# Attention and feed-forward on one core: block order, reciprocals in the products' bank, and a new order table

## The chip, the core and the metric

The kernel runs on one core of one Trainium2 chip. The metric is the device time of one execution in microseconds (us), lower is better. The core has a matrix engine (TensorE, PE in the profile, with its weight loads as PEld), a vector engine (VectorE, DVE), a scalar engine (ScalarE, ACT), a general engine (GpSimd, POOL) and a queue engine that issues the transfers (SyncE, SP). Each engine runs its own instructions in the order in which the program wrote them, and waits on semaphores for the others. Matrix products land in PSUM banks of 128 x 512 floats.

## What is computed

Causal attention in blocks of 64 positions over 8 batches, 8 heads, 576 positions and 64 dimensions, then a feed-forward layer with a SiLU over 4608 tokens (512 -> 2048 -> 512):

```python
scores = scale * np.matmul(q, k.transpose(0, 1, 3, 2))
mask = block_i >= block_j                     # blocks of 64 positions
scores = np.where(mask, scores, -1000000000.0)
attn = np.exp(scores - np.max(scores, axis=-1, keepdims=True))
attn = attn / (np.sum(attn, axis=-1, keepdims=True) + 1e-09)
attn_out = np.matmul(attn, v)
...
h = x @ w_in                                  # x: (4608, 512)
g = h * (1.0 / (1.0 + np.exp(-h)))
return (g @ w_out).astype(np.float32)
```

The feed-forward weights arrive as 64-bit words, which the kernel turns into 32-bit floats itself.

## The kernel before

**Precision.** Every operand of a large product is held as an upper part and a remainder (names ending in `hi` and `lo`); a product is three matmuls, or two where one side is left whole. ACT makes the upper parts, POOL mostly the remainders.

**Work items.** The feed-forward layer is cut into 18 blocks of 256 tokens. A step (block, d) has two items of 12 matmuls for the first layer (`ffn1`, line 599) and, two steps later, two items of 6 matmuls for the second (`ffn2`, line 629); between them ACT takes `silu` and `g_hi`, and POOL `g_lo`. The table's word `ffn` stands for one item. Blocks 0 and 1 hold the first 128 positions, which `First` (a, b) and `Second` (c0 to c3) attend to with small matmuls; while weights still come in, the two blocks alternate, `EVEN` times a step of each (`steps`, lines 657 to 659). Block 0 collects its output in PSUM bank S2 and in the bank U (line 622); both are needed by the units below.

**Weights.** 32 tiles w0 to w31: a transfer, `rebias` on ACT, three `bits` on DVE (lines 208, 212, 216), `hi` on ACT, `lo` on POOL.

**Units.** 64 units, one for a batch and head. `scores` fills the banks S0 to S2 (line 289); `max`, `max2` (DVE) find the row maxima; `sub` (DVE) subtracts them and so frees S0 to S2 for the next unit; `exp` and `p_hi` (ACT), `p_lo` (POOL); `sums` (DVE); `pv` multiplies by the values into the one bank U (line 370); `lower` (ACT) and `fold` (DVE, line 381) add its halves into `xu`. For a pair of units, at the odd one, `sums2` (DVE) makes the reciprocals `rr` and spreads them over 448 columns with a 32 x 32 transpose into `u.rb`, the upper half of the SBUF tile MR (lines 355 to 363); `mult` (line 384) multiplies `xu` by them, and `x_hi` (ACT, line 401) and `x_lo` (POOL, line 405) cut the result into the feed-forward tiles `x`. Block k from 4 on is ready once the last pair of the batches that it spans is.

**Order.** All of this is written into the engines' queues in one order. Up to unit 16 it is the table `ORDER`, one word for a method; 60 words `ffn` stand ahead of `u0.scores`, 152 in all. From unit 17 on the loop at line 722 takes over: in step i it writes `scores` and `max` of unit i, `fold` of unit i-2, `max2`, the splits of unit i+1, then for a pair `mult`, `x_hi`, `x_lo` of unit i-2, then `ffn(pace - 3)` (four items as a rule), `sums` and `pv` of unit i-1, the rest of unit i, and `ffn(3)`. After unit 63 nothing but feed-forward items is left.

Of the kernel before, what the change touches and what calls it, by code (L numbers as in the profile page):

```python
# [55 lines left out]
w2.hi w3.bits:2 w2.lo ffn w4.bits:0 w3.hi c0.load w4.bits:1 b.hi:0 w3.lo w5.rebias w7.load w4.bits:2 ffn b.hi:1 b.lo:0 w6.rebias
w8.load w5.bits:0 w4.hi ffn w5.bits:1 w4.lo b.lo:1 w5.bits:2 ffn silu w6.bits:0 g_hi w9.load w5.hi w6.bits:1 c0.scores:0 g_lo
w7.rebias w6.bits:2 ffn w7.bits:0 w5.lo w10.load silu w7.bits:1 w6.hi ffn w7.bits:2 w8.rebias w6.lo c0.max:0 w7.hi w11.load
w8.bits:0 ffn w9.rebias w8.bits:1 w7.lo g_hi w8.bits:2 ffn w10.rebias g_lo w9.bits:0 w8.hi w12.load w9.bits:1 ffn w8.lo w9.bits:2
c0.sub:0 w9.hi w13.load w10.bits:0 ffn silu w10.bits:1 w9.lo w11.rebias w10.bits:2 c0.scores:1 w12.rebias w11.bits:0 g_hi w14.load  # L60
ffn w10.hi w11.bits:1 w11.bits:2 w10.lo ffn w12.bits:0 w11.hi w15.load w12.bits:1 g_lo w13.rebias c0.max:1 ffn w12.bits:2 w11.lo
w14.rebias w13.bits:0 w12.hi w16.load ffn c0.sub:1 silu w13.bits:1 w12.lo w15.rebias ffn w13.bits:2 g_hi w14.bits:0 w13.hi
w17.load w14.bits:1 ffn w13.lo w14.bits:2 c0.exp w15.bits:0 ffn w18.load g_lo w15.bits:1 c0.sum ffn w15.bits:2 silu c0.norm ffn
w16.rebias w19.load w17.rebias w16.bits:0 w14.hi ffn g_hi w16.bits:1 w14.lo w16.bits:2 c0.turn:0 ffn w17.bits:0 g_lo w20.load
c0.back:0 w17.bits:1 w15.hi c1.load c0.turn:1 w18.rebias w17.bits:2 w15.lo ffn c0.back:1 w18.bits:0 w21.load w16.hi w18.bits:1
c0.pv silu w16.lo w18.bits:2 w19.rebias ffn g_hi w22.load w19.bits:0 w18.hi w17.hi w19.bits:1 ffn w20.rebias w19.bits:2 w17.lo
c0.hi w20.bits:0 w23.load ffn c0.lo g_lo w21.rebias w20.bits:1 w20.bits:2 c1.scores:0 w18.lo silu w21.bits:0 w19.hi w24.load ffn
w21.bits:1 w22.rebias w19.lo w21.bits:2 g_hi ffn w22.bits:0 w25.load g_lo w23.rebias w22.bits:1 w20.hi ffn w22.bits:2 w21.hi
w20.lo w23.bits:0 w22.hi w26.load w23.bits:1 ffn w21.lo w23.bits:2 w24.rebias silu ffn w24.bits:0 w22.lo w25.rebias w24.bits:1
g_hi ffn w24.bits:2 w26.rebias c1.max:0 w23.hi w28.load w25.bits:0 ffn w27.load w25.bits:1 w23.lo c1.sub:0 ffn w25.bits:2 g_lo  # L70
w26.bits:0 w29.load c1.scores:1 w26.bits:1 silu ffn g_hi c1.max:1 w24.hi g_lo w26.bits:2 w27.rebias ffn w27.bits:0 w30.load w24.lo
c1.sub:1 silu c1.load_v ffn w27.bits:1 w25.hi w26.hi w27.bits:2 w25.lo w28.rebias ffn w27.hi w31.load w28.bits:0 w26.lo w28.bits:1
ffn c1.exp w30.rebias ffn c1.sum g_hi w29.rebias g_lo ffn w28.bits:2 w29.bits:0 c1.norm ffn w29.bits:1 w29.bits:2 silu ffn
w30.bits:0 w29.hi w27.lo w30.bits:1 c1.turn:0 w30.bits:2 ffn c1.back:0 c3.load w30.hi c1.turn:1 c2.load ffn c1.back:1 w31.rebias
c1.pv w28.hi w31.bits:0 g_hi w28.lo ffn w31.bits:1 c1.hi c2.load_v w31.bits:2 g_lo c1.lo ffn silu c3.scores:0 w31.hi g_hi ffn
c3.max:0 g_lo c3.sub:0 c2.scores:0 w29.lo silu ffn c2.max:0 w30.lo c2.sub:0 c3.scores:1 ffn c3.max:1 c3.sub:1 c2.scores:1 ffn
c2.max:1 u0.load c3.exp c2.sub:1 ffn c3.load_v g_hi c3.sum c2.exp g_lo ffn c2.sum c3.norm ffn silu ffn g_hi c2.norm c3.turn:0 ffn
c3.back:0 u0.split_hi g_lo c3.turn:1 c2.turn:0 ffn w31.lo c2.back:0 c2.turn:1 ffn c2.back:1 c3.back:1 c2.pv ffn c2.hi u0.split_lo
c3.pv ffn c3.hi silu u1.load c3.lo ffn output c2.lo u0.load_v g_hi u0.scores g_lo output ffn mask u0.max silu u1.split_hi ffn g_hi
u0.max2 u0.v_hi g_lo ffn u1.split_lo silu ffn u0.sub ffn g_hi u2.load g_lo u1.scores store u0.exp:0 u0.v_lo u0.exp:1 ffn u1.max  # L80
u0.p_hi:0 store u0.exp:2 u0.p_lo:0 ffn u1.load_v u2.split_hi u1.max2 ffn u0.p_hi:1 u2.split_lo output ffn u1.sub silu ffn
u0.p_hi:2 u0.p_lo:1 output u0.sums u3.load g_hi u2.scores u0.p_lo:2 ffn g_lo u2.max u1.exp:0 u0.pv u1.exp:1 u3.split_hi u2.max2
ffn u1.exp:2 u3.split_lo u0.lower ffn u1.p_hi:0 u1.p_hi:1 u2.sub u1.v_hi ffn u1.v_lo u0.fold silu u3.scores u1.p_lo:0 u1.sums
u2.load_v g_hi u4.load u1.p_hi:2 u1.p_lo:1 ffn u3.max u1.p_lo:2 ffn u2.exp:0 g_lo u3.max2 u2.exp:1 u1.pv u2.exp:2 u4.split_hi ffn
u2.p_hi:0 u3.sub u4.split_lo u1.lower ffn u1.fold silu ffn u1.sums2 g_hi u2.p_lo:0 u5.load u2.p_hi:1 u4.scores u2.v_hi g_lo
u2.p_hi:2 ffn u2.p_lo:1 u1.mult silu u2.sums u1.x_hi u2.v_lo ffn u5.split_hi u2.p_lo:2 u3.load_v u4.max store ffn g_hi g_lo u2.pv
u4.max2 u3.exp:0 u1.x_lo u3.exp:1 ffn u3.exp:2 u3.p_hi:0 u5.split_lo u2.lower u3.sums ffn silu ffn u2.fold u3.p_hi:1 u3.p_lo:0
u4.sub u6.load g_hi u3.p_hi:2 ffn g_lo u3.v_hi u3.sums2 u5.scores u3.v_lo silu u3.p_lo:1 u4.load_v ffn u3.p_lo:2 u4.exp:0 u5.max
u6.split_hi ffn u4.exp:1 u6.split_lo u3.pv u4.exp:2 u5.max2 ffn u3.lower u4.p_hi:0 u3.fold u4.p_hi:1 ffn u7.load u4.p_lo:0 u5.sub
u4.v_hi u4.p_hi:2 store u4.v_lo ffn u3.mult u4.p_lo:1 u5.load_v u4.sums u6.scores u3.x_hi u4.p_lo:2 g_hi ffn u6.max u7.split_hi  # L90
g_lo u5.exp:0 ffn u5.exp:1 u3.x_lo u5.exp:2 u6.max2 u4.pv u7.split_lo ffn u5.p_hi:0 u6.sub u4.lower u5.p_hi:1 ffn u5.p_lo:0
# [713 lines left out]
```

## Time and profile before

| | |
|---|---|
| median of 3 runs | 1060.84 us (1060.02 to 1061.04) |
| profiled execution | 1061.71 us, of which the span from first to last instruction is 1060.0 us |
| PE busy | 1033.0 us (97%) |
| DVE, POOL, ACT busy | 792.0 us (75%), 750.6 us (71%), 746.3 us (70%) |
| granted TensorE clock | 0.992 of full speed over the span |

The program has four stretches. Until 26.8 us the first weights and a and b are made, and no feed-forward item has begun. From there to 133.5 us weights are turned and blocks 0 and 1 run. From 133.5 us to 319.75 us the table interleaves units 0 to 16 with items; after it comes the loop, and from 930 us on items alone. In the profile a busy PE need not be PE at its best: a matmul that waits for its operands while the one before it is still in flight is shown as a longer one. What PE lost is therefore read as the length of a stretch less the matmuls in it at their pace in an undisturbed stretch.

### The profile page before, as it was taken

Reading aid. Unit: us, or ns where it says so; the run is one execution under the profiler, and the core shown is the slowest. Engines: PE = TensorE matmul, PEld = TensorE weight load, DVE = VectorE, ACT = ScalarE, POOL = GpSimd, SP = SyncE. Lnnn points to the kernel's source line nnn. Section 1 sums busy time; section 2 is a strip of 40 time slices with the busy share of each in tenths; the row PEclk is TensorE's granted clock in tenths of the full one; section 3 lists DMA queues with packets and bytes.
Section 4 is the critical chain, followed back from the end, with each engine's and each line's share of the span. In section 5 each row is a group of like instructions: output and inputs, shape, how many; then the busy total and the mean of one; then the engine's idle time right before and its main releaser. Section 6 shows DMA issues by size and latency. Waiting matters only on the chain.

```text
span 1060.0 us, 19884 instructions
## 1 busy us (share of the span) xinstructions
PE 1033.0 (97%) x6996; PEld 930.3 (88%) x6996; DVE 792.0 (75%) x2238; ACT 746.3 (70%) x1193; POOL 750.6 (71%) x721
## 2 busy tenths in 40 slices
...
DMA packets 35043, 79.93 MB, mean 75 GB/s; under 512 B 4736, under 2 KB 12928, under 8 KB 34944
## 3 DMA queue, kind: packets, MB, share of 16 engines
...
## 4 chain that ended last, share of the span: by engine, by line
PE 77%; DVE 11%; POOL 4%; ACT 3%; DMA 3%; issue 2%; SPq 0%; DVEq 0%; POOLq 0%; ACTq 0%
PE h L599 31%; PE o L629 30%; PE S L289 7%; PE U L370 7%; DVE Mx L233 1%; DMA qkraw<-in_qk_dram 1%; DVE wm L216 1%; DVE S L212 1%; POOL pl L344 1%; DVE S L208 1%; DVE Dx L233 1%; DVE xu L384 1%; DMA wst<-in_moe_w_in_dram 1%; POOL ql L267 1%; POOL qh L265 1%
## 5 line engine op out<-in xcount | busy, mean ns | idle before, releaser
L599 PE MATMUL h<-x,wi 128*128 128x256 f32 x3456 | 440.5, 282 | 0.9 <-ACT g L606 0.9
L599 PEld LDWEIGHTS h<-x,wi 128*128 128x128 f32 x3456 | 429.0, 189 | 13.4 <-ACT g L606 2.7
L629 PE MATMUL o<-wo,g 128*128 128x512 f32 x1680 | 425.0, 398 | 2.7 <-ACT ot L637 2.7
L629 PEld LDWEIGHTS o<-wo,g 128*128 128x128 f32 x1680 | 305.9, 188 | 66.7 <-ACT ot L637 4.3
L344 POOL TENSOR_TENSOR pl<-p,ph 128x448 fp32r<-128x448 f32 (+1 forms) x192 | 227.2, 1209 | 85.5 <-ACT ph L336 85.5
L617 POOL TENSOR_TENSOR g<-g,g 128x512 fp32r<-128x512 f32 x144 | 186.2, 1293 | 127.9 <-ACT g L612 121.2
L233 DVE TRANSPOSE_TENSOR_REDUCE Mx<-S 64x4 f32<-64x128 f32 (+4 forms) x384 | 135.5, 404 | 76.6 <-PE S L289 76.1
L606 ACT ACTIVATE g<-h 128x512 f32<-128x512 f32 x144 | 86.0, 598 | 98.2 <-POOL g L617 56.8
L233 DVE TRANSPOSE_TENSOR_REDUCE Dx<-p 128x14 f32<-128x448 f32 (+3 forms) x320 | 123.3, 445 | 1.3 <-ACT p L330 1.2
L612 ACT CAST g<-g 128x512 fp32r<-128x512 f32 x144 | 89.3, 620 | 47.4 <-PE o L629 45.2
L330 ACT ACTIVATE p<-T 128x512 f32<-128x512 f32 (+1 forms) x192 | 105.0, 604 | 9.3 <-POOL ph L346 8.7
L265 POOL TENSOR_TENSOR qh<-qkraw,qh 64x576 fp32r<-64x576 f32 x64 | 95.2, 1488 | 17.9 <-ACT qh L261 10.9
L336 ACT CAST ph<-p 128x512 fp32r<-128x512 f32 (+1 forms) x192 | 104.2, 595 | 0.4 <-PE U L370 0.3
L289 PE MATMUL S<-qh 128*128 128x448 f32 (+3 forms) x320 | 92.6, 302 | 2.2 <-DVE T L319 1.0
L606 ACT ACT_TABLE_LOAD x66 | 84.7, 1283 | 1.2
L289 PE MATMUL S<-ql,qh 128*128 128x448 f32 (+3 forms) x320 | 84.1, 307 | 0.5 <-POOL ql L267 0.5
L330 ACT ACT_TABLE_LOAD x62 | 79.5, 1283 | 6.5 <-DVE Dx L233 5.3
L267 POOL TENSOR_TENSOR ql<-qkraw,qh 128x448 fp32r<-128x448 f32 x64 | 76.9, 1202 | 8.5 <-PE S L575 3.5
L401 ACT CAST x<-xu 128x256 fp32r<-128x256 f32 (+3 forms) x80 | 22.6, 339 | 81.7 <-DVE xu L384 81.7
L370 PE MATMUL U<-ph,vc 128*128 128x448 f32 (+3 forms) x320 | 74.6, 298 | 2.2 <-POOL vc L276 2.2
L321 DVE TENSOR_TENSOR T<-S,MR 128x256 f32<-128x256 f32 (+2 forms) x192 | 73.2, 408 | 0.0
L261 ACT CAST qh<-qkraw 128x1024 fp32r<-128x1024 f32 x64 | 66.8, 1044 | 2.8 <-DMA qkraw<-in_qk_dram 2.6
...
## 6 DMA issues: line engine op xcount, KB each, us to landing
qkraw<-in_qk_dram SPq DMA_DIRECT2D x128, 256.0 KB, 3.9
...
```

What stands on the lines that cost most here:

```text
L233: nc.vector.tensor_reduce(out=out, in_=in_, axis=AX.X, op=op, apply_transpose=True)
L265: nc.gpsimd.tensor_tensor(out=u.qh[64:, NQ:], in0=u.raw[64:, NQ:], in1=u.qh[64:, NQ:], op=ALU.subtract)
L289: nc.tensor.matmul(u.ps(c, w, m), u.kk[:, j * P : j * P + m], qq[:, q0 : q0 + w], start=i == 0, stop=i == 1)
L330: nc.scalar.activation(u.p[:, c:e], T[:, c:e], AF.Exp, scale=SCALE)
L336: nc.scalar.copy(u.ph[:, c:e], u.p[:, c:e])
L344: nc.gpsimd.tensor_tensor(out=u.pl[:, c:e], in0=u.p[:, c:e], in1=u.ph[:, c:e], op=ALU.subtract)
L370: nc.tensor.matmul(U[:m, q0 : q0 + w], u.vc[:, j, :m], (u.ph, u.pl)[pp][:, c : c + w], start=n == 0, stop=n == 8)
L599: nc.tensor.matmul(h[:, f, :], wi[wt][:, c, w], x[:, xt, :], start=n == 0, stop=n == 3 * CT - 1)
L606: nc.scalar.activation(g, hs.pop((blk, d)), AF.Silu)
L612: nc.scalar.copy(g2[:, 0], g)
L617: nc.gpsimd.tensor_tensor(out=g2[:, 1], in0=g, in1=g2[:, 0], op=ALU.subtract)
L629: nc.tensor.matmul(o, g2[:, gt, f, tk], wo[wt][:, 2 * d + f, :], start=d == 0 and n == 0, stop=d == NSTEP - 1 and n == 5,)
```

## The change

Four edits.

1. `EVEN` goes from 6 to 4: blocks 0 and 1 alternate for four steps each, then block 0 runs its last three steps on its own and block 1 follows. Block 0 is done two steps, or eight items, earlier.
2. `sums2` ends with the reciprocals. `mult` itself spreads them, into the bank U of the odd unit, whose products `fold` has just read, and multiplies `xu` by that bank.
3. The loop writes `mult` right behind `fold`, and `x_hi` and `x_lo` behind `ffn(pace - 3)` instead of ahead of it.
4. A new table `ORDER` with the same words, 152 `ffn` among them; 52 of these stand ahead of `u0.scores`, and the pairs follow one pattern.

```diff
-EVEN = 6
+EVEN = 4
...
 ORDER = """
-w0.load a.load b.load w1.load w0.rebias w0.bits:0 w0.bits:1 w0.bits:2 a.scores a.max:1 w3.load b.scores w2.load a.max:0 b.load_v
...
+w0.load a.load w1.load b.load w0.rebias w0.bits:0 w0.bits:1 w0.bits:2 a.scores w1.rebias w1.bits:0 w2.load a.max:1 a.max:0
...
         def sums2(u):
...
-            rr = sp.tile([P, NQB], F32, tag="rr", name="rr")
-            nc.vector.reciprocal(out=rr, in_=rs)
-            u.rb = MR[:, 512 : 512 + NQ]
-            bcast(u.rb, rr, NQB)
+            u.rr = sp.tile([P, NQB], F32, tag="rr", name="rr")
+            nc.vector.reciprocal(out=u.rr, in_=rs)
...
         def mult(u):
-            nc.vector.tensor_tensor(out=u.xu, in0=u.xu, in1=u.rb, op=ALU.mult)
+
+            bcast(u.U, u.rr, NQB)
+            nc.vector.tensor_tensor(out=u.xu, in0=u.xu, in1=u.U, op=ALU.mult)
...
         if z:
             z.fold()
+            if z.h % 2:
+                z.mult()
         if u:
             u.max2()
...
+        ffn(pace - 3)
         if z and z.h % 2:
-            z.mult()
             z.x_hi()
             z.x_lo()
-        ffn(pace - 3)
         if w:
             w.sums()
             w.pv()
```

**DVE at the start.** In the rows S_126 and S_225 (S_167 in the new program) are the scratch banks in which the bits of w0 and w1 are put together, U_131 and S_130 the scores of a, `o` those of b. Before:

```order
L216 SCALAR_TENSOR_TENSOR wm<-wst,S_126 128x512
L433 TENSOR_REDUCE m<-U_131 128x8
L433 TENSOR_REDUCE m<-S_130 128x8
L436 TENSOR_TENSOR p_132<-U_131,m 128x8x64
L436 TENSOR_TENSOR p_132<-S_130,m 128x8x64
L433 TENSOR_REDUCE m<-o 128x8
L208 TENSOR_SCALAR S_225<-wm 128x512
```

After:

```order
L216 SCALAR_TENSOR_TENSOR wm<-wst,S_126 128x512
L208 TENSOR_SCALAR S_167<-wm 128x512
L433 TENSOR_REDUCE m<-U_131 128x8
L433 TENSOR_REDUCE m<-S_130 128x8
L212 SCALAR_TENSOR_TENSOR S_167<-wst,S_167 128x512
L436 TENSOR_TENSOR p_132<-S_130,m 128x8x64
L436 TENSOR_TENSOR p_132<-U_131,m 128x8x64
```

The first operation on w1 now stands ahead of a's maxima on DVE; on SP the load of w1 moved from behind both halves of b to between a and b.

**ACT in the loop, where a block's output falls into a pair's step** (units 21 to 23). Before, with `x_hi` (line 401) ahead of the output copies (line 637) and of `silu` (line 606):

```order
L261 CAST qh<-qkraw 128x1024
L401 CAST x<-xu 128x128
L401 CAST x<-xu 128x256
L401 CAST x<-xu 128x64
L637 COPY ot<-o 128x512
L606 ACT_TABLE_LOAD
L606 ACTIVATE g<-h 128x512
```

After:

```order
L261 CAST qh<-qkraw 128x1024
L637 COPY ot<-o 128x512
L606 ACT_TABLE_LOAD
L606 ACTIVATE g<-h 128x512
L637 COPY ot<-o 128x512
L612 CAST g_5114<-g 128x512
L401 CAST x<-xu 128x128
```

The three casts of `x_hi` moved behind everything that the four items of that place need from ACT.

**POOL in the loop's first step** (unit 17; the x is that of unit 15). Before:

```order
L265 TENSOR_TENSOR qh<-qkraw,qh 64x576
L267 TENSOR_TENSOR ql<-qkraw,qh 128x448
L405 TENSOR_TENSOR x<-xu,x 128x64
L405 TENSOR_TENSOR x<-xu,x 128x256
L405 TENSOR_TENSOR x<-xu,x 128x128
L617 TENSOR_TENSOR g_4145<-g,g_4145 128x512
```

After:

```order
L265 TENSOR_TENSOR qh<-qkraw,qh 64x576
L267 TENSOR_TENSOR ql<-qkraw,qh 128x448
L617 TENSOR_TENSOR g_4139<-g,g_4139 128x512
L405 TENSOR_TENSOR x<-xu,x 128x64
L405 TENSOR_TENSOR x<-xu,x 128x256
```

The remainders of x moved behind one `g_lo` (line 617). The first of them, 64 columns wide, belongs to block 5, whose first item is the fifth of this step.

## Rows read from the trace of the kernel before

**Rows 1.** The page: busy time, share of the span and instructions.
```profile
PE 1033.0 (97%) x6996; PEld 930.3 (88%) x6996; DVE 792.0 (75%) x2238; ACT 746.3 (70%) x1193; POOL 750.6 (71%) x721
```

**Rows 2.** Three stretches: length, each engine's busy time, clock, DMA share, GB/s.
```profile
26.80:133.50 106.70, 103.63 (x845) 91.31 (x841) 77.61 (x120) 71.55 (x114) 65.98 (x51) 1.00 0.60 183
133.50:319.75 186.25, 181.30 (x1143) 160.80 (x1142) 175.42 (x539) 155.67 (x250) 161.63 (x160) 1.00 0.27 72
...
420.00:800.00 380.00, 380.00 (x2453) 346.29 (x2453) 325.84 (x979) 299.69 (x477) 310.08 (x301) 1.00 0.25 64
```

**Rows 3.** First matmul of unit 0's, unit 16's and unit 17's scores in the timeline.
```profile
133.51 0.37 PE L289 MATMUL S<-qh 128*128 128x448 f32 x1
...
302.77 0.37 PE L289 MATMUL S<-qh 128*128 128x448 f32 x1
...
319.75 0.37 PE L289 MATMUL S<-qh 128*128 128x448 f32 x1
```

**Rows 4.** The chain that ended last, in order of time: start, us, what.
```profile
104.84 1.02 PE S L557 x16
...
122.78 0.87 PE S L457 x8
...
126.91 1.10 PE S L575 x32
...
310.15 2.81 PE o L629 x12
```

**Rows 5.** The timeline at the start: start, us, engine, line, operation.
```profile
9.06 0.69 DVE L433 TENSOR_REDUCE m<-U 128x8 f32<-128x512 f32 x1 [1.34 <-PE U L505]
9.29 1.13 PE L505 MATMUL o<-qk 64*64 64x64 f32 x32 [0.28 <-DMA qk<-in_qk_dram]
...
11.89 0.66 ACT L200 ACTIVATE wm<-wst 128x512 f32<-128x512 f32 x1 [6.34 <-DMA wst<-in_moe_w_in_dram]
...
21.12 1.21 DVE L450 TENSOR_TENSOR T<-T,rr 128x1024 f32<-128x1024 f32 x1
...
26.79 5.90 PE L599 MATMUL h<-x,wi 128*128 128x256 f32 x48
```

**Rows 6.** DVE's groups by line and shape: busy us, mean ns, idle before.
```profile
L384 DVE TENSOR_TENSOR xu<-xu,MR 128x448 f32<-128x448 f32 x32 | 40.8, 1276 | 0.1
L319 DVE TENSOR_TENSOR T<-S,MR 128x448 f32<-128x448 f32 x64 | 38.9, 607 | 1.5
L237 DVE STREAM_TRANSPOSE MR<-rr 128x448 f32<-128x448 f32 x32 | 20.6, 645 | 1.1
```

**Rows 7.** Line 384 alone: duration in ns, least, median and most.
```profile
L384 DVE TENSOR_TENSOR xu<-xu,MR x32: 581/1344/1836, 170.9 to 930.7; 128x448 f32<-128x448 f32 x32
```

**Rows 8.** PE's waits over 320 to 930 us: total, times, longest.
```profile
PE o L629 <- ACT ot L637: 2.7, 4, 0.7
PE h L599 <- ACT g L606: 0.9, 1, 0.9
```

**Rows 9.** The timeline of unit 23's step, where two of these waits fall.
```profile
395.84 0.37 PE L289 MATMUL S<-qh 128*128 128x448 f32 x1
...
398.89 0.63 DVE L381 TENSOR_TENSOR xu<-U,t 64x448 f32<-64x448 f32 x1
...
402.98 0.60 PE L370 MATMUL U<-ph,vc 128*128 128x448 f32 x3
...
403.81 0.75 ACT L401 CAST x<-xu 128x128 fp32r<-128x128 f32 x3 [4.87 <-DVE xu L384]
...
405.09 1.66 PE L629 MATMUL o<-wo,g 128*128 128x512 f32 x6 [0.61 <-ACT ot L637]
```

**Rows 10.** The timeline of unit 17's step, around the first item of block 5.
```profile
328.21 2.98 PE L599 MATMUL h<-x,wi 128*128 128x256 f32 x24
...
328.55 1.44 POOL L405 TENSOR_TENSOR x<-xu,x 128x64 fp32r<-128x64 f32 x3
...
329.95 1.30 POOL L617 TENSOR_TENSOR g<-g,g 128x512 fp32r<-128x512 f32 x1
```

More of the change, by code (lines that the diff above doesn't have):

```diff
@@ L56 @@
[L56 to L91, printed above, removed]
@@ L104 @@
-u11.exp:0 u11.load_v u10.pv u12.max2 u11.exp:1 u11.exp:2 u9.x_hi ffn u11.p_hi:0 u11.sums u9.x_lo u14.load g_hi ffn u10.lower
-u11.p_hi:1 u11.p_lo:0 u11.v_hi u10.fold ffn u11.p_hi:2 u12.sub u11.p_lo:1 ffn u11.v_lo u11.sums2 u12.exp:0 u11.p_lo:2 u13.scores
-u12.load_v u12.exp:1 g_lo ffn u12.exp:2 u14.split_hi u13.max u11.pv u14.split_lo ffn u13.max2 silu u11.lower g_hi ffn u12.v_hi
-g_lo u12.p_hi:0 u11.fold u11.mult ffn output u12.v_lo u13.sub silu u12.p_lo:0 u12.p_hi:1 ffn u13.load_v u12.p_hi:2 u15.load
@@ L108 @@
-u12.p_lo:1 g_hi u12.sums u11.x_hi u14.scores store u12.p_lo:2 output ffn u14.max g_lo u12.pv u13.exp:0 u11.x_lo u15.split_hi
-u14.max2 ffn u13.exp:1 u15.split_lo u13.exp:2 u13.p_hi:0 ffn u12.lower u14.sub u13.p_hi:1 ffn u13.p_lo:0 u16.load u12.fold silu
-u15.scores u13.p_lo:1 u13.sums u13.p_hi:2 u13.v_hi u13.p_lo:2 ffn u15.max u13.v_lo ffn u14.exp:0 u15.max2 u14.load_v g_hi u13.pv
-u14.exp:1 g_lo u16.split_hi ffn u14.exp:2 u13.sums2 u16.split_lo ffn silu g_hi ffn u13.lower u15.sub g_lo u17.load u14.p_hi:0
@@ new lines @@
+u2.load_v u4.split_hi output ffn u3.max u4.split_lo output u2.exp:1 u1.pv u2.exp:2 u3.max2 ffn silu u5.load g_hi ffn u2.p_hi:0
+g_lo u3.sub u1.lower u2.p_hi:1 ffn u2.p_lo:0 silu u1.fold u4.scores u2.p_lo:1 u2.sums g_hi u2.p_hi:2 u2.v_hi ffn u2.p_lo:2 u4.max
+ffn u2.v_lo u3.exp:0 g_lo u1.mult u3.exp:1 ffn u3.load_v u5.split_hi u4.max2 u2.pv u3.exp:2 u5.split_lo ffn silu u4.sub u1.x_hi
+ffn u2.lower u6.load u1.x_lo u3.p_hi:0 u3.sums ffn u3.p_hi:1 u3.p_hi:2 u3.p_lo:0 u3.v_hi u5.scores g_hi u2.fold u3.p_lo:1 u3.sums2
```

80 lines of the change are left out of this document (60 added, 20 removed).

## The prediction

> **What bounds the kernel now.** The page comes first: PE is busy 97% of the span, no other engine over 75% [rows 1]. The change leaves the number of matmuls as it is, so the most it can give back is what PE loses. The table of stretches says where that is. From 420 to 800 us PE is busy all of the 380 us, with DVE at 325.84 of 380, 86% [rows 2]; that is the undisturbed pace. An item takes 2.81 / 2 = 1.405 us there [rows 4], and a step of the loop (seven items, one `scores`, one `pv`) takes (395.84 - 319.75) / 6 = 12.68 us [rows 3, 9], so `scores` and `pv` together 12.68 - 7 x 1.405 = 2.85 us. By these prices:
>
> - From the first item (26.79 us, [rows 5]) to unit 0 (133.51 us, [rows 3]) are 106.7 us. The 60 items take 84.3; c0 to c3 take 4 x (2 x 1.02 + 0.87 + 1.10) = 16.0 on PE [rows 4]. PE loses 6.4 us.
> - From unit 0 to unit 17 (319.75 us, [rows 3]) are 186.2 us. The 92 items take 129.3, 17 `scores` and 16 `pv` about 47.1, together 176.4. PE loses 9.8 us, with DVE busy 175.42 of 186.25, 94% [rows 2]: here DVE sets the pace.
> - From 320 us on PE waits 2.7 us for output copies and 0.9 us for a `silu`, 3.6 in all [rows 8].
>
> The sum below is made against the profiled execution: 1061.71 us, a span of 1060.0 and 1.7 around it, and 0.87 above the median, which is taken off at the end.
>
> **Edit 1 and the table: what stands ahead of unit 0.** Block 0 holds two of the banks that unit 0 needs, so unit 0 can't begin ahead of block 0's end. With `EVEN` at 4 that is eight items, 11.2 us, earlier. This is no gain in itself: the eight items now lie between unit 0 and unit 17. What it does is give the stretch that DVE paces more PE work to lie beside.
>
> **The start gets longer.** DVE takes a's first maximum at 9.06 us [rows 5]. In the new order the first operation on w1 stands ahead of it. w1 is now the fourth half-megabyte on the queue; the fourth of before, b's first half, let its scores begin at 9.29. `rebias` adds 0.66 [rows 5], the operation itself about 0.7, so a's maximum begins near 10.65, 1.6 us later. Between there and the end of b's normalisation (21.12 + 1.21 = 22.33 us, [rows 5]) the new order has five bit operations on DVE instead of four, 0.7 more; a few tenths more or less of idle time are likely. I take +2.5 us for the first item: 29.3 us. Bounds: +1.0, if w1 lands a little sooner and the extra operation fills idle time, and +3.5, if every gap there adds.
>
> **To unit 0.** 52 items are 73.1, c0 to c3 16.0, the loss 6.4 as before: unit 0 at 29.3 + 95.5 = 124.8 us. The loss here can be 4 (PE begins later while DVE has nearly kept its place) or 9 (weights are wanted earlier, since the last steps of block 0 now follow each other); DVE has room, 77.61 of 106.70 us [rows 2].
>
> **Edit 2: the product.** With both inputs in SBUF it takes 1276 ns on average [rows 6], but 581 at its best and 1836 at its worst [rows 7]: half and more is waiting. The nearest row with one input in PSUM and 448 columns is line 319 with 607 ns [rows 6]. I take 607, so 0.67 us a pair; the spread stays at 645 ns [rows 6], now with its output in a bank, for which the trace has no row of this operation; its other DVE operations write banks at their usual time, so I allow 0 to +0.3 us. Seven products lie between units 0 and 17: DVE's 175.4 us become 170.7. [...]
>
> **Unit 0 to unit 17.** 100 items are 140.5, with 47.1 as before 187.6 us. DVE's share falls from 94% to 170.7 / 187.6 = 91%. PE loses 9.8 us at 94% and nothing at 86%. In proportion 91% would cost 6.0; waits rise faster than in proportion near the top, so I take half, 4.9. Bounds 1 and 9.8. Unit 17 begins at 124.8 + 187.6 + 4.9 = 317.3 us, 2.4 earlier than now.
>
> **Edit 3: the loop.** In unit 23's step ACT stands idle for 4.87 us until DVE has the product, and only then copies the output that PE waits for [rows 9]. In the new order the copies and `silu` come first, so the 3.6 us of [rows 8] go: both waits have this one cause, and nothing else there was late, since PE's next operands are ready while it waits. In exchange two places get tighter. Block 5 begins at unit 17's step (328.21 us) and block 12 at unit 49's, each with the fifth item of its step, and need the pair's x. POOL made its first remainder at 328.55, 0.34 us into the item, and `g_lo` only at 329.95 [rows 10]. Behind a `g_lo` of 1.30 us it is later by that much less the earlier start of ACT; the item reaches the part with this x after 9 of its 12 matmuls, 1.1 us in. I take 0.65 us lost at each, 1.3 together; bounds 0 and 2.6. Net for the loop: -2.3 us.
>
> DVE's order costs the loop nothing: the spread and the product come ahead of `max2`, 1.25 us, where before the product stood behind it with 1.28. The bank U is held 1.25 us longer. In unit 23's step `fold` ends at 399.52 and PE comes to the next `pv` at 402.98 [rows 9]: 3.5 us, so 2.2 remain. `x_lo` ends later, and the next `fold` into `xu` is a step away.
>
> **Sum.** 1061.71 - 2.4 - 2.3 = 1057.0 for a profiled execution, less 0.87: **1056 us**.
>
> **Rivals.**
> - *DVE no longer limits.* Losses of 4 and 1 us instead of 6.4 and 9.8, and no new wait in the loop: 2.5 - 2.4 - 8.8 - 3.6 = -12.3, 1049 us. For it: POOL and ACT stand at 87% and 84% in that stretch [rows 2], and 91% is not far from the loop's free 86%. Against: four engines in one order, each waiting for the others.
> - *Nothing gained ahead of the loop.* The loss from unit 0 to 17 stays near 9.8, because the waits pass to POOL or ACT: 2.5 + 0 - 2.3 = +0.2, 1061 us.
> - *The product gets no cheaper.* The change then doesn't do what it says. DVE keeps 175.4 of 187.6 us, 93.5%, so a loss near 9: 2.5 - 0.8 - 2.3 = -0.6, 1060 us. [...] Against it stand 607 and 581 ns [rows 6, 7].
> - *Slower: PE waits at the bank U.* In the table three items, 4.2 us, lie between `u4.scores` and `u2.pv`; DVE has `u2.sums`, `u4.max` and now the spread and product of unit 1 to do in that time, and `pv` can't begin before. There are eight such places. If each costs the whole 1.25 us, it is 2.5 - 4.9 + 10.0 - 2.3 = +5.3, 1066 us. It makes the kernel slower by 0.2% from 0.85 us a place on. For it: before, `pv` waited only for `fold`. Against: a DVE that is in step with PE has done it.
>
> **How the numbers follow.** About 0.2%, 2.1 us, is what a measurement of this kernel can tell from no change. Chances: the forecast 0.50, DVE no longer limiting 0.18, nothing gained ahead of the loop 0.12, the product no cheaper 0.06, the bank U 0.14. The first two are faster: 0.68. The next two lie within 0.2%: 0.18. The last is slower: 0.14. The forecast's own bounds (start 1.0 to 3.5, loop 0 to 2.6) make it 1052 to 1059; the range goes on to 1049 for the first rival and to 1062 for the middle ones, and leaves out most of the bank U: **1049 to 1062**.
>
> **What would show it.** Line 384 near 0.61 us with the bank U as input. First item near 29.3 us, unit 0 near 125, unit 17 near 317. No wait of PE for line 637 between 320 and 930 us, none of ACT for the product; a short wait at the first item of block 5 and of block 12. The prediction is wrong if PE waits at line 370 for the product, if the first item comes before 28 or after 31 us, or if unit 17 begins after 320 us.

## The result and the profile after

The changed kernel takes 1050.12 us (median of 4 runs, 1049.66 to 1050.99) against 1060.8 before on the same chip: a ratio of 0.9902, interval [0.9884, 0.9919]. It is 10.7 us faster, where 4.8 were forecast. The profiled execution is 1050.03 us long, its span 1048.3 (before 1061.71 and 1060.0).

The page of the changed kernel, and three stretches of its table (columns as in [rows 2]): ahead of unit 0, unit 0 to 17, and the undisturbed stretch.

```profile
PE 1027.9 (98%) x6996; PEld 931.2 (89%) x6996; DVE 767.1 (73%) x2238; ACT 750.5 (72%) x1195; POOL 741.4 (71%) x721
```

```profile
28.06:122.09 94.03, 92.31 (x777) 81.04 (x769) 76.06 (x118) 68.16 (x108) 65.32 (x53) 1.00 0.66 208
122.09:312.95 190.86, 189.09 (x1215) 171.56 (x1214) 170.84 (x538) 162.25 (x257) 162.84 (x159) 1.00 0.29 71
312.95:1048.30 735.35, 731.61 (x4707) 665.54 (x4705) 500.46 (x1551) 507.72 (x812) 509.67 (x499) 1.00 0.20 54
420.00:800.00 380.00, 379.72 (x2451) 346.45 (x2451) 314.61 (x978) 301.32 (x478) 303.31 (x299) 1.00 0.25 64
```

PE has the same 6996 matmuls; DVE is 24.9 us less busy than in [rows 1], and in the undisturbed stretch it falls from 325.84 to 314.61 us [rows 2]. The timeline of the changed kernel, at the places of [rows 3]:

```profile
122.09 0.37 PE L289 MATMUL S<-qh 128*128 128x448 f32 x1
...
289.08 0.37 PE L289 MATMUL S<-qh 128*128 128x448 f32 x1
...
312.95 0.36 PE L289 MATMUL S<-qh 128*128 128x448 f32 x1
```

With the first item at 28.1 us (before 26.8), the account reads:

| stretch | before, us | after, us | forecast, us | PE's loss before | after | forecast |
|---|---|---|---|---|---|---|
| start to first item | 26.8 | 28.1 | 29.3 | | | |
| first item to unit 0 | 106.7 | 94.0 | 95.5 | 6.4 | 4.9 | 6.4 |
| unit 0 to unit 17 | 186.2 | 190.9 | 192.5 | 9.8 | 3.3 | 4.9 |
| unit 17 to the end | 740.25 | 735.35 | 737.95 | | | |

What PE lost is the length less the prediction's own prices: 52 items and c0 to c3 are 89.1 us, 100 items with the units 187.6. The second and the third row together are 8.1 us better (293.0 to 284.9), the loop is 4.9 better, and the start 1.3 worse.

The product, by DVE's groups and by line 384 alone (answers to [rows 6, 7]):

```profile
L384 DVE TENSOR_TENSOR xu<-xu,U 128x448 f32<-128x448 f32 x32 | 19.9, 620 | 1.1
L237 DVE STREAM_TRANSPOSE U<-rr 128x448 f32<-128x448 f32 x32 | 20.8, 649 | 0.9
```

```profile
L384 DVE TENSOR_TENSOR xu<-xu,U x32: 620/620/622, 164.1 to 919.0; 128x448 f32<-128x448 f32 x32
```

The mean falls from 1276 to 620 ns, and the spread of durations from 1255 ns to 2: its length no longer depends on what stands beside it. Its best case of before, 581 ns, was shorter.

Unit 23's step in the changed kernel (timeline, answer to [rows 9]):

```profile
389.26 0.37 PE L289 MATMUL S<-qh 128*128 128x448 f32 x1
...
392.33 0.59 ACT L637 COPY ot<-o 128x512 f32<-128x512 f32 x1
...
393.65 0.62 DVE L384 TENSOR_TENSOR xu<-xu,U 128x448 f32<-128x448 f32 x1
...
395.69 0.58 ACT L637 COPY ot<-o 128x512 f32<-128x512 f32 x1
396.35 0.61 PE L368 MATMUL U<-ph,vc 128*128 128x448 f32 x3
396.67 0.76 ACT L401 CAST x<-xu 128x128 fp32r<-128x128 f32 x3
...
397.68 2.97 PE L629 MATMUL o<-wo,g 128*128 128x512 f32 x12
```

The copies come ahead of the casts, PE takes line 629 without a wait, and the step is 12.66 us long instead of 14.57. The product ends at 394.27, 2.08 us ahead of the `pv` that needs the bank U, and 2.06 to 2.08 us ahead of it in all the odd steps of the loop. PE's waits over the whole loop (columns as in [rows 8]) shrink from two kinds to one, and over units 0 to 17 the bank U shows up:

```profile
PE h L599 <- POOL x L405: 0.3, 1, 0.3
```

```profile
PE U L368 <- DVE xu L384: 1.3, 3, 0.9
PE U L368 <- POOL g L617: 0.2, 1, 0.2
```

### The profile page after: what moved, and what is told of

Its sections match the earlier page's. It is cut to its first block, busy times and chain, and to the rows that moved or that the text cites. A ratio compares the mean times of both kernels' runs of the same rounds, so it can differ in the third digit from the quotient of the medians.

```text
span 1048.3 us, 19893 instructions
## 1 busy us (share of the span) xinstructions
PE 1027.9 (98%) x6996; PEld 931.2 (89%) x6996; DVE 767.1 (73%) x2238; ACT 750.5 (72%) x1195; POOL 741.4 (71%) x721
## 3 DMA queue, kind: packets, MB, share of 16 engines
q1 hardware_dynamic: 34944, 78.66, 26.8%
## 4 chain that ended last, share of the span: by engine, by line
PE 82%; DVE 7%; ACT 4%; POOL 3%; issue 2%; DMA 2%; SPq 0%; DVEq 0%; ACTq 0%; POOLq 0%
PE o L629 33%; PE h L599 33%; PE S L289 7%; PE U L368 7%; DVE wm L216 1%; DVE Dx L233 1%; DVE S L212 1%; DMA qkraw<-in_qk_dram 1%; DVE S L208 1%; DVE Mx L233 1%; POOL pl L344 1%; DMA wst<-in_moe_w_in_dram 1%; ACT p L330 1%; PE S L629 1%; ACT g L606 0%
## 5 line engine op out<-in xcount | busy, mean ns | idle before, releaser
L265 POOL TENSOR_TENSOR qh<-qkraw,qh 64x576 fp32r<-64x576 f32 x64 | 91.5, 1430 | 15.3 <-ACT qh L261 10.7
L267 POOL TENSOR_TENSOR ql<-qkraw,qh 128x448 fp32r<-128x448 f32 x64 | 74.1, 1158 | 5.0
L276 POOL TENSOR_TENSOR vc<-vraw,vc 128x320 fp32r<-128x320 f32 x64 | 56.6, 884 | 13.9 <-ACT vc L273 13.4
```

Source lines behind the costliest of these rows:

```text
L265: nc.gpsimd.tensor_tensor(out=u.qh[64:, NQ:], in0=u.raw[64:, NQ:], in1=u.qh[64:, NQ:], op=ALU.subtract)
```

## The experiments

The same stretches were read in every kernel from the first matmul of an item, of unit 0 and of unit 17, in one profiled execution each; times in us, the ratio to the runs of before on the same chip, whose medians are 1060.78 to 1061.37 us.

| kernel | median | ratio, interval | first item | to unit 0 | unit 0 to 17 | unit 17 to end |
|---|---|---|---|---|---|---|
| before | 1060.84 | | 26.8 | 106.7 | 186.24 | 740.25 |
| changed | 1050.12 | 0.9902 [0.9884, 0.9919] | 28.1 | 94.0 | 190.86 | 735.35 |
| e1_table_only | 1055.92 | 0.9954 [0.9938, 0.9971] | 27.6 | 94.1 | 192.06 | 739.88 |
| e2_product_loop_only | 1053.14 | 0.9925 [0.991, 0.994] | 25.9 | 107.1 | 182.86 | 735.30 |
| e3_x_early | 1049.96 | 0.9895 [0.988, 0.991] | 28.7 | 94.0 | 191.04 | 734.56 |
| e4_product_in_sbuf | 1052.38 | 0.9919 [0.9904, 0.9933] | 29.6 | 93.8 | 192.16 | 735.64 |
| e5_before_x_later | 1057.77 | 0.9965 [0.9952, 0.9978] | 27.2 | 105.8 | 186.11 | 736.23 |
| e7_spread_twice | 1054.52 | 0.9937 [0.9922, 0.9951] | 28.5 | 94.0 | 194.77 | 735.37 |
| e8_before_product_in_bank | 1065.98 | 1.0045 [1.0029, 1.0062] | 26.3 | 106.5 | 182.99 | 748.16 |
| e9_x_early_start | 1049.38 | 0.9892 [0.9877, 0.9906] | 28.3 | 94.0 | 191.35 | 734.56 |
| e10_x_early_again | 1049.68 | 0.9894 [0.9877, 0.991] | 28.5 | 94.0 | 191.26 | 734.56 |
| e11_before_spread_late | 1061.32 | 1.0 [0.9991, 1.001] | 26.8 | 107.3 | 185.64 | 740.17 |
| e12_spread_behind | 1053.13 | 0.9919 [0.9903, 0.9936] | 29.4 | 93.8 | 192.83 | 735.39 |

### The two halves of the change

**e1_table_only**: the kernel before with `EVEN = 4` and the new table, nothing else.

```diff
-EVEN = 6
+EVEN = 4
...
 ORDER = """
...
```

> The kernel before with the new table and EVEN = 4 alone: the product stays in SBUF, the loop stays as it was. Theory A (the gain is two parts that add: what the table saves ahead of unit 17, and what the loop saves behind it; the cheaper product is a small share of the first): the stretch from unit 17 to the end keeps its 740.2 us with the long steps of units 23 and 55 (14.6 us), unit 17 begins near 315, 2 us later than with all edits, and the time is near 1056. Rival B (the table is only as good as the cheaper product lets it be, DVE still sets the pace): unit 17 begins at 318 or later, 1059 or more.

Measured 1055.92 us, as the first theory said. The stretch from unit 0 to 17 is 192.06 us, a loss of 4.5, though the product still takes two SBUF inputs. The loop keeps its waits (740.25 to 739.88). `EVEN` and the order of the new table were not tried apart.

**e2_product_loop_only**: the kernel before with edits 2 and 3, and the old table.

```diff
...
+            bcast(u.U, u.rr, NQB)
+            nc.vector.tensor_tensor(out=u.xu, in0=u.xu, in1=u.U, op=ALU.mult)
...
             z.fold()
+            if z.h % 2:
+                z.mult()
...
+        ffn(pace - 3)
         if z and z.h % 2:
-            z.mult()
             z.x_hi()
             z.x_lo()
-        ffn(pace - 3)
```

> The old table and EVEN = 6, with the product in the bank and the new loop. Theory A: from unit 17 to the end 735.4 us as with all edits (steps of units 23 and 55 at 12.7), unit 17 begins 2 to 3 us earlier than before (DVE paces that stretch and saves 4.7 us in it), near 317: 1053.5. Rival B: the whole 4.7 us come back ahead of unit 17 (315.0): 1051. Rival C: the loop's gain hangs on the table too, and the long steps stay: 1058.

Measured 1053.14 us. The loop gains 5.0 us here, as in the changed kernel, and unit 0 to 17 another 3.4. The two halves give 5.3 and 8.1 us alone (against the runs of before on their own chip) and 10.7 together, so they overlap. The place is between units 0 and 17: PE's loss falls there by 5.3 and 3.4 us alone and by 6.5 together, so about 2.2 us are the same gain.

### Which part of edit 3 removes the stall

**e3_x_early**: the changed kernel with the casts ahead of the items again; the product stays early.

```diff
-        ffn(pace - 3)
         if z and z.h % 2:
             z.x_hi()
             z.x_lo()
+        ffn(pace - 3)
```

> All edits, but in the loop x_hi and x_lo stand ahead of ffn(pace - 3) again; the product stays right behind fold. Theory A (ACT only has to be free in time; the early product is enough): ACT waits some 2 us for the product in each pair's step instead of 4.9, the steps of units 23 and 55 stay at 12.7, and the short losses at block 5 and block 12 (0.15 and 0.55 us) go: 1049.4. Rival B (the place of x_hi is what counts): the two long steps come back with 1.9 us each: 1053.

Measured 1049.96 us: with an early product nothing is lost by the casts' place. Between 320 and 930 us ACT's waits for the product are 24.8 us with a longest of 2.9, where before they were 74.6 and 4.9; PE has no wait at all there, and the steps of units 17 and 49 fall from 12.83 and 13.22 us to 12.68 each. The rival is out.

**e5_before_x_later**: the reverse. In the kernel before, only the casts and POOL's remainders of x move behind the items; the product stays late.

```diff
         if z and z.h % 2:
             z.mult()
+        ffn(pace - 3)
+        if z and z.h % 2:
             z.x_hi()
             z.x_lo()
-        ffn(pace - 3)
```

> The kernel before with one thing moved: in the loop, x_hi and x_lo stand behind ffn(pace - 3) instead of ahead of it. The product stays where it was, behind the splits, with both inputs in SBUF; the table is the old one. Theory A (the stall in the loop is only that ACT waits for the product ahead of the output copies; it costs what the long steps are longer, not what the wait rows say): the stretch ahead of unit 17 stays as before (unit 0 to unit 17 about 186.2 us); the steps of units 23 and 55 go from 14.6 to about 12.7 us; unit 17 to the end goes from 740.25 to about 736 us, with some loss at the first item of blocks 5 and 12, where the late product now makes x still later; time about 1057 us. Rival B (the product itself has to come earlier as well): the steps stay near 14.6 us or the loss passes to the first items of blocks 5 and 12, 2 us and more at each; time 1060 us or more.

Measured 1057.77 us, theory A. The long steps of units 23 and 55 are 12.69 us each, so the place of the casts, ahead of the copies, was the whole stall. In the timeline of unit 23's step the copies now come ahead of a product that is as late as before:

```profile
399.09 0.59 ACT L637 COPY ot<-o 128x512 f32<-128x512 f32 x1
...
402.10 1.84 DVE L384 TENSOR_TENSOR xu<-xu,MR 128x448 f32<-128x448 f32 x1
402.48 0.58 ACT L637 COPY ot<-o 128x512 f32<-128x512 f32 x1
...
403.98 0.75 ACT L401 CAST x<-xu 128x128 fp32r<-128x128 f32 x3 [0.40 <-DVE xu L384]
```

The price is paid at blocks 5 and 12, whose first items wait for x: the steps of units 17 and 49 are 13.52 and 13.51 us, 0.8 longer. So either half of edit 3 removes the stall. The early product does it for nothing (e3_x_early, where the other edits are in place), the late casts at a price; the changed kernel has both and pays 0.15 and 0.55 us there (steps of 12.83 and 13.22 us). The second of these in the changed kernel's timeline:

```profile
728.62 1.42 POOL L405 TENSOR_TENSOR x<-xu,x 128x64 fp32r<-128x64 f32 x3
...
728.98 1.92 PE L599 MATMUL h<-x,wi 128*128 128x256 f32 x14 [0.28 <-POOL x L405]
```

PE is idle for 0.28 us, and begins the part with this x 0.36 us after POOL has begun the first remainder.

### What edit 2 is worth, and when it costs

**e4_product_in_sbuf**: the changed kernel with edit 2 undone. The spread is back in `sums2`, into the SBUF tile, and the product keeps its new place.

```diff
...
-            bcast(u.U, u.rr, NQB)
-            nc.vector.tensor_tensor(out=u.xu, in0=u.xu, in1=u.U, op=ALU.mult)
+            nc.vector.tensor_tensor(out=u.xu, in0=u.xu, in1=u.rb, op=ALU.mult)
```

> All edits but the second: the reciprocals are spread into SBUF by sums2, and the product has two SBUF inputs, at the new place behind fold. Theory A: line 384 back near 1.28 us, 21 us more of DVE in all; no PE loss in the loop, where DVE has room (86%), and about 2 us between unit 0 and unit 17: 1052. Rival B: DVE sets the pace of that stretch, all 4.7 us come back: 1055. Rival C: no difference there, 1050.

Measured 1052.38 us, near theory A in time, but not by its price: DVE is busy 775.1 us, 8.0 more than in the changed kernel and not 21. Of the 2.9 us between the two profiled executions (1052.92 and 1050.03) 1.3 lie between units 0 and 17, 0.3 in the loop, and the rest in that execution's start. Up to unit 17 this kernel is e1_table_only, and e3_x_early and e10_x_early_again are the changed kernel: 192.06 and 192.16 us with the product in SBUF, 190.86 to 191.26 with the bank, so about 1.1 us. With two SBUF inputs the product is at 574/723/1158 ns (least, median, most), in e1_table_only, with its late place in the loop, at 574/1148/1835, and before at 581/1344/1836 [rows 7]. The earlier place takes most of the excess out of the median, and POOL, whose busy time goes back to 751.3 us, pays for it (last section).

**e8_before_product_in_bank**: the kernel before with edit 2 alone; `mult` stays behind `max2` and the splits.

```diff
         def sums2(u):
...
-            u.rb = MR[:, 512 : 512 + NQ]
-            bcast(u.rb, rr, NQB)
...
         def mult(u):
-            nc.vector.tensor_tensor(out=u.xu, in0=u.xu, in1=u.rb, op=ALU.mult)
+            bcast(u.U, u.rr, NQB)
+            nc.vector.tensor_tensor(out=u.xu, in0=u.xu, in1=u.U, op=ALU.mult)
```

> The kernel before with edit 2 alone: the spread is made by mult, into the bank U, and the product reads that bank; mult stands where it stood, behind max2 and the splits, with x_hi and x_lo right behind it, and the table is the old one. Theory A (edit 2 gives DVE time between units 0 and 17 and does nothing for the stall in the loop, since the spread and the product together take as long as the old product did at that place): line 384 near 0.62 us; unit 0 to unit 17 from 186.24 to about 183 us; the steps of units 23 and 55 stay near 14.5 us; unit 17 to the end about 740 us; time about 1057.5 us. Rival B (the cheap product also ends ACT's wait earlier): the two long steps shrink too, unit 17 to the end about 737 us, time 1054 to 1055 us. Rival C (edit 2 does nothing by itself): 1060 to 1061 us.

Measured 1065.98 us, 0.45% slower than before, which none of the three had. Unit 0 to 17 is 182.99 us, as theory A said. But the loop is 7.9 us longer: every odd step but two (units 23 and 55, 13.98 each) is 13.12 to 13.17 us instead of 12.64 to 12.73. PE's waits between 320 and 930 us begin with

```profile
PE U L368 <- DVE xu L384: 3.7, 16, 0.2
```

and unit 25's step shows the place in the timeline:

```profile
426.03 0.62 DVE L237 STREAM_TRANSPOSE U<-rr 128x448 f32<-128x448 f32 x1
426.69 0.62 DVE L384 TENSOR_TENSOR xu<-xu,U 128x448 f32<-128x448 f32 x1
...
427.45 0.68 PE L368 MATMUL U<-ph,vc 128*128 128x448 f32 x3 [0.25 <-DVE xu L384]
```

The product ends at 427.31 and `pv` follows at 427.45. Counted from the step's `scores` that is 7.50 us; in the kernel before `pv` came after 7.09. The rows say 0.2 us a time, the steps 0.45 to 0.5.

**e11_before_spread_late** settles whether the bank or DVE's order is the cause: the same moved spread, but into the SBUF tile.

```diff
             u.rb = MR[:, 512 : 512 + NQ]
-            bcast(u.rb, rr, NQB)
...
         def mult(u):
+            bcast(u.rb, u.rr, NQB)
             nc.vector.tensor_tensor(out=u.xu, in0=u.xu, in1=u.rb, op=ALU.mult)
```

> The kernel before with the spread moved from sums2 to mult, as in e8_before_product_in_bank, but still into the SBUF tile: DVE has the same order of operations as there, the product is even longer, and the bank U isn't held by it. It tells why that run was slower than before. Theory A (there PE's pv waited for the bank U): the odd steps of the loop are 12.65 to 12.7 us, as before, and not 13.13; units 23 and 55 near 15.2 us, since ACT gets the product 0.65 us later than before; unit 17 to the end about 742 us, time about 1062 us. Rival B (the later spread makes DVE late, whatever it writes to): the odd steps are 13.1 us and more, unit 17 to the end 748 us and more, time 1069 us.

Measured 1061.32 us, a ratio of 1.0. The odd steps are back at 12.64 to 12.73 us, but for units 23 and 55, so DVE's order is innocent and the bank U is the cause. Unit 25's step in this kernel's timeline:

```profile
430.13 1.03 DVE L384 TENSOR_TENSOR xu<-xu,MR 128x448 f32<-128x448 f32 x1
...
430.49 0.60 PE L369 MATMUL U<-ph,vc 128*128 128x448 f32 x3
```

The product ends at 431.16, 0.67 us after `pv` has begun, and PE's rows show no wait for it. One figure was missed: the steps of units 23 and 55 are 14.48 and 14.44 us, not 15.2: in unit 23's step the product begins 0.63 us later than before, but takes 1.14 us instead of 1.83.

### DVE's time and the bank between units 0 and 17

**e7_spread_twice** and **e12_spread_behind** both add one more spread for each pair to the changed kernel: the first ahead of the product, into the bank U, the second behind it, into SBUF.

```diff
             bcast(u.U, u.rr, NQB)
+            bcast(u.U, u.rr, NQB)
             nc.vector.tensor_tensor(out=u.xu, in0=u.xu, in1=u.U, op=ALU.mult)
```

```diff
             bcast(u.U, u.rr, NQB)
             nc.vector.tensor_tensor(out=u.xu, in0=u.xu, in1=u.U, op=ALU.mult)
+            bcast(MR[:, 512 : 512 + NQ], u.rr, NQB)
```

> The changed kernel with the spread of the reciprocals into the bank U made twice, one behind the other (the second writes the same numbers): 0.65 us more on DVE for each pair, and the bank U is held that much longer. Theory A (between units 0 and 17 DVE's own time still passes to the end nearly one for one, as 1.5 us of it did when the product was put back into SBUF; in the loop the bank has 2.2 us of slack): unit 0 to unit 17 goes from 190.9 to about 194 us (7 x 0.65 = 4.5 us of DVE, most of it paid), unit 17 to the end stays at 735 to 736 us; time about 1053.5 us. Rival B (DVE no longer limits): nothing changes, 1050 us. Rival C (the bank U is what PE waits for): pv waits for the product at most of the 32 pairs, in the loop too, 0.65 us each, 8 us and more in the loop and on the page a wait of PE at line 368 for line 385 of that size; time 1060 us or more.

> The changed kernel with a second spread, behind the product and into a part of an SBUF tile that nothing reads: the same 0.65 us more on DVE for each pair as in e7_spread_twice, but the bank U is free when the product ends, as in the changed kernel. Theory A (between units 0 and 17 it is DVE's own time that is paid): unit 0 to unit 17 about 194.5 us, as in that run (194.77), time about 1054 us. Rival B (most of the 3.9 us there was PE at the bank U): unit 0 to unit 17 about 192 us or less, time about 1051.5 us. Unit 17 to the end stays at 735 to 736 us by both.

The first measured 1054.52 us, unit 0 to 17 194.77 (+3.9 on 190.86); the second 1053.13 us and 192.83 (+2.0), between its two theories. Unit 17 to the end is 735.4 us in both: in the loop 0.65 us more on the bank or on DVE costs nothing. Between units 0 and 17 DVE's busy time grows from 170.84 to 175.46 us in the first and to 174.33 in the second, so 3.9 of 4.6 us reach the end there, and 2.0 of 3.5 here: DVE's time is paid in part, and more of it where the bank is held as well. PE's waits there, of the first and then of the second:

```profile
PE U L368 <- DVE xu L385: 3.5, 4, 0.9
PE U L368 <- POOL qh L265: 1.3, 1, 1.3
PE U L368 <- ACT p L330: 0.9, 1, 0.9
```

```profile
PE U L368 <- DVE xu L384: 3.0, 5, 0.7
PE U L368 <- POOL qh L265: 0.6, 1, 0.6
```

The bank's waits grow in both, from 1.3 us in the changed kernel and 2.0 to 2.1 in e3, e9 and e10, which have the same program between these units. That stretch is 190.86 to 191.35 us long in these four executions, so the 3.9 and 2.0 us are known to about half a microsecond. That the waits grow in the second as well, since a later DVE also comes later to the next pair, was argued and not shown, and how the 3.9 us divide between the two causes stays open.

### The start

**e9_x_early_start** is e3_x_early with the first operation on w1 behind a's two maxima; **e10_x_early_again** is e3_x_early once more, on the same chip.

```diff
-... a.scores w1.rebias w1.bits:0 w2.load a.max:1 a.max:0
-w1.bits:1 b.scores ...
+... a.scores w1.rebias w2.load a.max:1 a.max:0
+w1.bits:0 w1.bits:1 b.scores ...
```

> The changed kernel with two things put back: x_hi and x_lo stand ahead of ffn(pace - 3) in the loop, and in the table w1.bits:0 stands behind a's two maxima instead of ahead of them. Theory A (the first operation on w1 costs a's chain its own 0.7 us and the wait for w1's rebias): a's first maximum begins near 9 us instead of 10.31, the first item 0.6 to 1.2 us earlier on the mean than in the changed kernel, everything behind it unchanged; time about 1049 us, the same as the run beside it less 0.7. Rival B (the weights set when the first items can run, or the scatter of the start, 27.6 to 29.6 us in four executions of one start, covers it): no difference from the run beside it, 1050 us.

> The changed kernel with x_hi and x_lo ahead of ffn(pace - 3) again, as in the run named e3_x_early, on the same chip as the run with the other start. Expected 1050.0 us (1049.96 there), the first item between 27.6 and 29.6 us.

Measured 1049.38 and 1049.68 us, which can't be told apart. a's first maximum begins at 9.02 us instead of 10.66, but b's normalisation ends at 23.80 instead of 23.99, and the first item begins at 28.3 instead of 28.5: 1.6 us at the head of DVE's queue are 0.2 us at its end. The time is rival B's, but the rows give another reason than it did (next section, the start).

## Why the prediction was too small

**What bounds the kernel: right.** PE's matmuls stayed what they were, and the gain is in what PE loses. Two steps of the working failed. The stall in the loop was priced by PE's wait rows: net 2.3 us, measured 4.9, the largest miss. And PE's loss between units 0 and 17 was read off DVE's busy share: 4.9 us, measured 3.3. The time lies outside the forecast's own bounds, 1052 to 1059 us; that it is inside the range is owed to the room left for the first rival.

**The first rival, DVE no longer limiting: near by luck.** Its 1049 us are the nearest figure. But it had losses of 4 and 1 us ahead of the loop, where 4.9 and 3.3 were left; a start 1.2 us too long and a gain in the loop 1.3 us too small made up most of that. And DVE still limits in part: in e7_spread_twice and e12_spread_behind more work on it between units 0 and 17 is paid.

**The start: right in kind, 1.2 us too dear (0.5 on the mean).** Forecast +2.5 us, measured +1.3 in the profiled executions. One execution tells little here: the five with the old start have their first item at 25.9 to 27.2 us, the seven with the new one at 27.6 to 29.6, on the mean 26.6 and 28.6, so the table costs 2.0 us. Nearly all of it is there at a's first maximum, as forecast: it begins at 8.25 to 9.07 us in the five and at 9.73 to 10.92 in the seven, 1.8 later on the mean, behind the operation on w1 (changed kernel's timeline, beside [rows 5]):

```profile
9.71 0.69 DVE L208 TENSOR_SCALAR S<-wm 128x512 uint32<-128x512 uint32 x1 [2.11 <-ACT wm L200]
10.31 0.68 DVE L433 TENSOR_REDUCE m<-U 128x8 f32<-128x512 f32 x1
```

The term that fell is the 0.7 us for a fifth bit operation: from a's maximum to the end of b's normalisation are 13.15 to 13.56 us in the old order and 13.33 to 13.37 in the new one, so it filled idle time, as the lower bound had it. e9_x_early_start gives a's maximum its place back (9.02 us) and still ends b's normalisation at 23.80, against 22.33 before. Its rows say why: the operation on w1 now stands between the two, so six bit operations do, and in this execution a's normalisation, which takes 1.21 us before and in the changed kernel, falls beside POOL's remainders of w0 and w1:

```profile
16.31 2.49 POOL L227 TENSOR_TENSOR wi<-wm,wi 128x512 fp32r<-128x512 f32 x2 [14.54 <-ACT wi L224]
17.96 1.92 DVE L450 TENSOR_TENSOR p<-p,rr 128x1024 f32<-128x1024 f32 x1
```

**To unit 0: 1.5 us better than forecast.** The loss went from 6.4 to 4.9 us, inside the bounds of 4 to 9; I had let it stand. It is a property of the table, 93.8 to 94.1 us in eight executions. The nearest row is one of PE's waits ahead of unit 0, at line 457 in c's chain for POOL, which I had not taken up. PE's waits on this way are 3.1 us in all before and 1.8 in the changed kernel, which has 1.0 us of a new kind, at line 557 for DVE. Before, and then in the changed kernel:

```profile
PE S L457 <- POOL MR L450: 1.5, 1, 1.5
```

```profile
PE S L457 <- POOL MR L450: 0.3, 1, 0.3
```

It was not tried alone.

**The product: right as a price, lucky as a sum.** 620 ns for 607, the spread 649 for 645, and DVE's time between units 0 and 17 is 170.84 us where I had 170.7. But the forecast's whole saving of 4.7 us was to come from edit 2, and the new table alone brings DVE there to 172.31 us. The seven products of that stretch before, in e1_table_only and in the changed kernel:

```profile
L384 DVE TENSOR_TENSOR xu<-xu,MR 128x448 f32<-128x448 f32 x7 | 8.3, 1179 | 0.1
L384 DVE TENSOR_TENSOR xu<-xu,MR 128x448 f32<-128x448 f32 x7 | 4.6, 653 | 0.0
L384 DVE TENSOR_TENSOR xu<-xu,U 128x448 f32<-128x448 f32 x7 | 4.3, 621 | 0.2
```

With the new order most of the waiting is out of the product before its input moves; I had taken the old mean as the price at any place. In the new table edit 2 takes 0.2 us off the seven products, and one spread more falls into the loop (seven in the stretch instead of eight). In the old table (e2_product_loop_only) it takes 3.9 us off them.

The rival that the product gets no cheaper is out as a time. With one input in the bank the product takes 620 ns, against 574 to 581 at best with both in SBUF (before, e1_table_only, e4_product_in_sbuf), so its best case got dearer. What decides is how far it goes above that. e8_before_product_in_bank and e11_before_spread_late have the same order of operations: with the bank the product is at 620/621/622 ns (least, median, most), with two SBUF inputs at 625/1131/1607. POOL lost by it too (last section). In unit 25's step of the kernel before, the product takes 1.64 us and POOL's line 267, which begins before it ends, 1.43; in the next step, which has no product, line 267 takes 1.16 (timeline):

```profile
428.91 1.43 POOL L265 TENSOR_TENSOR qh<-qkraw,qh 64x576 fp32r<-64x576 f32 x1
429.19 1.64 DVE L384 TENSOR_TENSOR xu<-xu,MR 128x448 f32<-128x448 f32 x1
430.42 1.43 POOL L267 TENSOR_TENSOR ql<-qkraw,qh 128x448 fp32r<-128x448 f32 x1
...
442.66 1.16 POOL L267 TENSOR_TENSOR ql<-qkraw,qh 128x448 fp32r<-128x448 f32 x1
```

**Unit 0 to 17: 1.6 us too little, and the method fell.** I turned DVE's share into a loss, and took waits to rise faster than in proportion near the top. The stretches of the experiments say that there is no such curve: a share of 93.0% (170.09 of 182.86) loses 6.5 us in e2_product_loop_only, 90.1% (175.46 of 194.77) loses 7.2 in e7_spread_twice, 90.4% (174.33 of 192.83) 5.2 in e12_spread_behind, and 89.5 to 89.7% lose 3.3 to 4.6 in the changed kernel, e1_table_only and e4_product_in_sbuf. The shares that I compared were not of one kind either: 94% and 86% are of whole stretches, 91% is of a stretch without its loss (of the forecast 192.5 us it would be 89%). The new table, with its eight items more in the stretch and its other order, was worth more than the cheaper product: with the product still in SBUF the loss is already 4.5 us (e1_table_only), where I had priced that rival at 9 by "93.5%, so a loss near 9". Single waits tell more than the share. Before, PE's largest one in this stretch was for POOL's part of the values; e2_product_loop_only still has it with 2.2 us, e1_table_only with 0.8, and in the changed kernel it is gone, so it went with the table and the rest of it with edit 2:

```profile
PE U L370 <- POOL vc L276: 2.2, 2, 1.8
```

What is left in e1_table_only is all of PE's waiting for POOL there:

```profile
PE U L370 <- POOL vc L276: 0.8, 2, 0.6
PE U L370 <- POOL ph L346: 0.7, 1, 0.7
PE S L289 <- POOL ql L267: 0.7, 1, 0.7
```

With edit 2 POOL is busy 162.84 us in the stretch instead of 165.72, and these waits shrink from 2.2 us to 0.2. So what edit 2 gives there in the new table goes along with a shorter POOL far more than with a shorter product.

**The loop: mechanism right, stall too cheap.** Forecast -3.6 + 1.3, measured -4.9. I took PE's wait rows [rows 8] as the price. They say 1.33 us for unit 23's step; the step was 14.57 us long beside neighbours of 12.68, so 1.9. More of it stands in the rows of the weight loads of the same step, which I had not read as its price:

```profile
PEld o L629 <- ACT ot L637: 2.1, 2, 1.2
```

Two such steps give 3.8 us, three shorter stalls (units 36, 40, 52) 0.65, the `silu` behind unit 63 another 1.3: 5.7 in all. Of the 1.3 us for blocks 5 and 12, 0.7 came (0.15 and 0.55), and by e3_x_early they were not needed.

**The bank U: the rival exists, but is small here.** I gave it 2.2 us of slack in the loop; it has 2.08. In units 0 to 17 it takes 1.3 us in three waits, and 2.0 to 2.1 us in e3, e9 and e10; that PE waits for the product there is one of the signs that I had named for being wrong. It is e8_before_product_in_bank that shows the danger: edit 2 at the product's old place, and the kernel is slower than before. Edit 2 needs edit 3 (edit 3 keeps its gain in the loop without edit 2, e4_product_in_sbuf), which the prediction said nowhere: it looked at the bank's slack at the new place alone.

In sum, of the 6.9 us between the profiled forecast (1057.0) and 1050.03, the start gives 1.2, the way to unit 0 1.5, units 0 to 17 1.6, and the loop 2.6.

## What to carry to other kernels

Price a stall that you mean to remove by the length of its step against its neighbours', and read the weight loads' waits beside the matmuls': neither is the price by itself (1.33 and 2.1 us for a step that was 1.9 us longer). Before a buffer gets a second use, ask when its next owner comes: edit 2 was worth 3.3 us in one stretch of the old table and cost 8 in another, and only its place in the queue turned that round. An engine's busy share says where to look, not what a stretch loses. And the price of an operation that is lengthened by a neighbour holds for its place alone: the new order by itself brought seven products from 8.3 us to 4.6.

## What the runs showed of the chip

Without the product's two SBUF inputs POOL's own operations got shorter, though nothing of them changed. POOL's groups of the kernel before and then of the changed one:

```profile
L265 POOL TENSOR_TENSOR qh<-qkraw,qh 64x576 fp32r<-64x576 f32 x64 | 95.2, 1488 | 17.9 <-ACT qh L261 10.9 <-issue 2.7 <-POOL g L617 0.2
L267 POOL TENSOR_TENSOR ql<-qkraw,qh 128x448 fp32r<-128x448 f32 x64 | 76.9, 1202 | 8.5 <-PE S L575 3.5
```

```profile
L265 POOL TENSOR_TENSOR qh<-qkraw,qh 64x576 fp32r<-64x576 f32 x64 | 91.5, 1430 | 15.3 <-ACT qh L261 10.7 <-POOL g L617 0.3
L267 POOL TENSOR_TENSOR ql<-qkraw,qh 128x448 fp32r<-128x448 f32 x64 | 74.1, 1158 | 5.0
```

These are 6.5 us of POOL's 9.2 us between [rows 1] and the page after. It is the product's inputs that decide: POOL is busy 749.8 to 751.3 us in the five kernels with the product in SBUF (before, e1, e4, e5, e11) and 741.4 to 742.2 in the eight with the bank, whatever the order. The cleanest pair is e11 and e8, with the same order of operations: 750.0 and 741.8 us. The order chose who was hit. In e4_product_in_sbuf the two lines above are at 1452 and 1157 ns, and another pays:

```profile
L346 POOL TENSOR_TENSOR ph<-p,ph 64x64 fp32r<-64x64 f32 x64 | 27.5, 429 | 5.0
```

In the changed kernel that line takes 318 ns. Between units 0 and 17 in the new table it is POOL that pays for the product in SBUF: 2.6 to 2.9 us more, while the products themselves are 0.2 us longer. No run parts the share of POOL in edit 2's gain there from that of the spread which falls into the loop.
